# A two-layer attention and FFN kernel: residual kept token-major, layernorm transposed by DMA, heads spread over the partitions, attention weights spread by selector matmuls

## The chip, the cores and the metric

The kernel runs on one core of one Trainium2 chip. The metric is the time of one execution on the device, in microseconds (us). "Median" is the median over the runs of one kernel. "Span" is the time from the first to the last instruction in the one profiled execution, which is some 1 to 2 us shorter than the time of that run.

Engines in the profile: PE is TensorE's matmuls, PEld its weight loads (they overlap PE), DVE is VectorE, ACT is ScalarE, POOL is GpSimd, SP is SyncE, which here only starts DMAs.

## The reference

Two layers. Each is a sliding-window attention block followed by an FFN, each with a layernorm in front and a residual around it. There are 2048 tokens, width 1024, 32 heads of 32, a window of 8 keys at distances 0, 2, ..., 14, and an FFN width of 3584. Everything is bf16.

```python
def _A_ref(x, wqkv, wo):                       # B=1, S=2048, D=1024, H=32, Dh=32
    qkv = (x @ wqkv).reshape(B, S, 3, H, Dh).transpose(2, 0, 3, 1, 4)
    q, k, v = qkv[0], qkv[1], qkv[2]
    idx = pos[:, None] - (jnp.arange(8) * 2)[None, :]
    # kg, vg: rows idx of k and v; idx < 0 is masked
    logits = einsum("bhsd,bhswd->bhsw", q, kg) * Dh ** -0.5
    o = einsum("bhsw,bhswd->bhsd", softmax(logits), vg)
    return o.transpose(0, 2, 1, 3).reshape(B, S, D) @ wo

def _B_ref(x, w1, b1, w2, b2):                 # F=3584
    return gelu(x @ w1 + b1) @ w2 + b2

for layer in range(2):                         # written out twice in the reference
    x = x + _A_ref(layernorm(x), A_wqkv, A_wo)
    x = x + _B_ref(layernorm(x), ...)
```

## The kernel before

Tokens go through in groups of 512. There are four groups and two layers, so eight steps `n`. The program is a software pipeline: the attention of step `n` is spread as "sides" between the FFN matmuls of step `n-1`.

The residual `xg` is feature-major: features lie on the partitions and tokens along the free axis. Three things follow. The input must be transposed by TensorE. The output must be transposed back. And the mean and the variance of a token are sums over partitions, which the kernel makes with matmuls against a tile of ones:

```python
def load_x_tile(g, tl):                        # input: 8 identity transposes on TensorE
    ...
    for c in range(KD):
        m = tr(pst[:, c, :], xin[:, c * P:(c + 1) * P], ident[:])
    nc.scalar.copy(xg[g][:, :, tl * P:(tl + 1) * P], pst[:])
# store_x_tile does the same on the way out

class LN:
    def s1a(self):                             # the mean
        if self.presum: ...                    # 8 planes added on VectorE first, then one matmul
        else:
            for c in range(KD):
                m = mm(self.tot[...], lhsT=ones_bf[:], rhs=x[:, c, ...], start=(c == 0), stop=(c == KD - 1))
    # s1b subtracts the mean; s2a squares on ScalarE and sums again with ones_bf; s3 multiplies by rstd
```

The columns of Q, K and V come in the order of the weights, so a 128-row chunk `c` holds four whole heads. The product of the attention weights with V therefore needs, for each chunk, a tile in which the weights of each of its four heads stand on 32 partitions. The kernel writes the weights to DRAM and reads them back by broadcast DMAs, 1 MB for each chunk, issued from GpSimd and tied to TensorE's progress:

```python
def av_a(n, c):
    ...
    for hi in range(HPC):                      # 4 DMAs of 256 KB for each chunk
        src = a_d[HPC * c + hi:HPC * c + hi + 1, :, :].rearrange("o w t -> o (w t)").to_broadcast([DH, W * T])
        d = ABC_Q.dma_start(abc[hi * DH:(hi + 1) * DH, :, :].rearrange("p w t -> p (w t)"), src)
        if mark[0] is not None:
            dep_sync(d, mark[0], "pace abc broadcast with PE progress")
    nc.vector.tensor_tensor(out=abc[:], in0=abc[:], in1=win(vT[:, c, :]), op=ALU.mult)
# av_b_dve then adds the 8 window positions in three halving steps into oT[:, c, :]
```

One AV chunk is placed every five chunks of FFN1 (in the last of the eight steps, every three):

```python
u_list = [1 + 5 * c for c in range(NCH)]
# ... sides of gen_ffn1(n - 1); the last two chunks go into gen_ffn2(n - 1)
```

Of the kernel before, what the change touches and what calls it, by code (L numbers as in the profile page):

```python
# [8 lines left out]
ACT = mybir.ActivationFunctionType  # L9
# [5 lines left out]
DRAM = bass.MemoryType.DRAM  # L15
# [3 lines left out]
def kernel(  # L19
# [11 lines left out]
):  # L31
    nc = tc.nc
# [12 lines left out]
    NQ = 4  # L45
    TB = T // NQ
    NTT = T // P
    assert DH == 32 and P // DH == 4 and H * NQ == P
    assert S % T == 0 and D % (4 * P) == 0 and F % (4 * P) == 0
# [3 lines left out]
    KH = KF // 2  # L53
    HPC = P // DH
    NCH = D // P
    NSTEP = NLAYER * NG
    LN_SET = "natural_log_exp_and_others"
    N_FFN1 = KF
    N_FFN2 = (KD // 2) * 4
    N_QKV = 3 * NCH  # L60
# [4 lines left out]
    wo_v = A_wo.rearrange("(k p) f -> p k f", p=P)  # L65
# [5 lines left out]
    wpool = ctx.enter_context(tc.tile_pool(name="wpool", bufs=4))  # L71
    lnp = ctx.enter_context(tc.tile_pool(name="lnp", bufs=1))
    xnp = ctx.enter_context(tc.tile_pool(name="xnp", bufs=2))
    attp = ctx.enter_context(tc.tile_pool(name="attp", bufs=1))
    qp = ctx.enter_context(tc.tile_pool(name="qp", bufs=2))
    prodp = ctx.enter_context(tc.tile_pool(name="prodp", bufs=3))
    smp = ctx.enter_context(tc.tile_pool(name="smp", bufs=1))
    abcp = ctx.enter_context(tc.tile_pool(name="abcp", bufs=3))
    iop = ctx.enter_context(tc.tile_pool(name="iop", bufs=2))
    psum = ctx.enter_context(tc.tile_pool(name="psum", bufs=1, space=PSUM))  # L80
    dram = ctx.enter_context(tc.tile_pool(name="dram", bufs=2, space=DRAM))
    pools = {"hpool": None, "abcx": None, "abcx_cm": None}

    def acc_tile():
        return psum.tile([P, T], F32, name="acc", bufs=4)

    def aux_f32():
        return psum.tile([P, T], F32, name="aux", bufs=2)

    def aux_tr():  # L90
        return psum.tile([P, KD, P], BF16, name="aux", bufs=2)

    def dep_sync(dependent, dependency, why):
        tc.add_manual_dep(dependent.ins, dependency.ins.name,
                          mybir.DependencyInfo(mybir.DependencyClass.Sync, mybir.DependencyReason.SCHED_ONLY), reason=why)
# [5 lines left out]
    last_pe = [None]  # L101
    mark = [None]

    ABC_Q = nc.gpsimd

    PIN_MODE = 0
    VFIRST = False
    PE_AV = False
    ONE_AHEAD = True
    RED_BATCH = 2  # L110
    PRESUM = True
    PRESUM_B = False
    DMA_XPOSE = False
    OT_BUFS = 1 if ONE_AHEAD else 2
    LN_TILED = False
    last_seg = [None]

    def pe_chain(inst, seg):
        if last_pe[0] is not None:
            if PIN_MODE == 1 or (PIN_MODE == 2 and seg != last_seg[0]):  # L120
                dep_order(inst, last_pe[0], "PE program order")
        last_pe[0] = inst
        last_seg[0] = seg
        return inst

    def _seg(out_ap):
        return (out_ap.tensor.name, out_ap.offset)

    def mm(out_ap, *args, **kwargs):
        return pe_chain(nc.tensor.matmul(out_ap, *args, **kwargs), _seg(out_ap))  # L130

    def tr(out_ap, *args, **kwargs):
        return pe_chain(nc.tensor.transpose(out_ap, *args, **kwargs), out_ap.tensor.name)  # L133

    xg = [xpool.tile([P, KD, T], BF16, name=f"xg{g}") for g in range(NG)]
    def load_x(g):
        d = nc.sync.dma_start_transpose(xg[g][:], x_in[g * T:(g + 1) * T, :].rearrange("s (k p) -> s k p", p=P))
        if mark[0] is not None:
            dep_sync(d, mark[0], "keep the x load at its program position")

    def load_x_tile(g, tl):
        xin = iop.tile([P, D], BF16, name="xio")
        d = nc.sync.dma_start(xin[:], x_in[g * T + tl * P:g * T + (tl + 1) * P, :])
        if mark[0] is not None:
            dep_sync(d, mark[0], "keep the x load at its program position")
        pst = aux_tr()
        for c in range(KD):
            m = tr(pst[:, c, :], xin[:, c * P:(c + 1) * P], ident[:])
            if c == 0 and mark[0] is not None:
                dep_order(m, mark[0], "keep the input transposes at their program position")  # L150
        nc.scalar.copy(xg[g][:, :, tl * P:(tl + 1) * P], pst[:])

    if DMA_XPOSE:
        load_x(0)

    ident = const.tile([P, P], BF16, name="ident")
    make_identity(nc, ident[:])
    ones_bf = const.tile([P, P], BF16, name="ones_bf")
    nc.vector.memset(ones_bf[:], 1.0)
    eps_t = const.tile([P, 1], F32, name="eps_t")  # L160
    nc.vector.memset(eps_t[:], EPS)
    q32 = const.tile([P, P], BF16, name="q32")
    nc.vector.memset(q32[:], 1.0 / 32.0)
    smat = const.tile([P, NCH, H], BF16, name="smat")
    nc.gpsimd.memset(smat[:], 0.0)
    for c in range(NCH):
        for hi in range(HPC):
            m = HPC * c + hi
            nc.gpsimd.memset(smat[hi * DH:(hi + 1) * DH, c, m:m + 1], 1.0)
    maskrow = const.tile([1, W, 16], BF16, name="maskrow")  # L170
    nc.gpsimd.memset(maskrow[:], 0.0)
    for wp_ in range(W):
        nmask = HALO - DIL * wp_
        if nmask > 0:
            nc.gpsimd.memset(maskrow[0:1, wp_, 0:nmask], -1e9)
    onesrow = const.tile([1, H], BF16, name="onesrow")
    nc.gpsimd.memset(onesrow[:], 1.0)
    b1_bf = const.tile([P, KF], BF16, name="b1_bf")
    b2_bf = const.tile([P, KD], BF16, name="b2_bf")
    b1T = const.tile([P, KF], F32, name="b1T")  # L180
    b2T = const.tile([P, KD], F32, name="b2T")

    def load_bias():
        with nc.allow_non_contiguous_dma(reason="tiny bias loads"):
            d1 = nc.gpsimd.dma_start(b1_bf[:], B_b1.rearrange("(j p) -> p j", p=P))
            d2 = nc.gpsimd.dma_start(b2_bf[:], B_b2.rearrange("(j p) -> p j", p=P))
        if mark[0] is not None:
            dep_sync(d1, mark[0], "keep the bias load at its program position")
            dep_sync(d2, mark[0], "keep the bias load at its program position")
        nc.vector.tensor_copy(b1T[:], b1_bf[:])  # L190
        nc.vector.tensor_copy(b2T[:], b2_bf[:])
# [3 lines left out]
    nc.gpsimd.memset(zhalo[:], 0.0)  # L195

    def store_x_tile(g, tl):
        pst = aux_tr()
        for c in range(KD):
            tr(pst[:, c, :], xg[g][:, c, tl * P:(tl + 1) * P], ident[:])  # L200
        xo = iop.tile([P, D], BF16, name="xio")
        nc.scalar.copy(xo[:], pst[:].rearrange("p c t -> p (c t)"))  # L202
        nc.sync.dma_start(out_v[g * T + tl * P:g * T + (tl + 1) * P, :], xo[:])

    def rstd_from(src, prev, preload, c0=0, c1=T):
        rstd = lnp.tile([P, T], F32, name="rstd", bufs=2)
        if preload:
            pl = nc.scalar.preload_act_table_set(LN_SET)
            dep_order(pl, prev, "table preload after squares")
            prev = pl  # L210
        ln_i = nc.scalar.activation(rstd[:, c0:c1], src, ACT.Ln, bias=eps_t[:], scale=1.0 / D)
        dep_order(ln_i, prev, "ln after squares/preload")
        nc.scalar.activation(rstd[:, c0:c1], rstd[:, c0:c1], ACT.Exp, scale=-0.5)  # L213
        return rstd

    class LN:
        def __init__(self, g, preload=False, cols=None, xn=None, presum=False):
            self.g = g
            self.xn = xn
            self.preload = preload  # L220
            self.presum = presum
            self.c0, self.c1 = cols if cols is not None else (0, T)

        def _pin(self, m):
            if mark[0] is not None:
                dep_order(m, mark[0], "keep LN matmuls at their program position")

        def _partial(self, rhs_of):
            c0, c1 = self.c0, self.c1
            pq = aux_f32()  # L230
            for c in range(KD):
                j = c % 4
                m = mm(pq[j * 32:(j + 1) * 32, c0:c1], lhsT=ones_bf[:, 0:32], rhs=rhs_of(c),
                       start=(c < 4), stop=(c >= KD - 4), tile_position=(0, j * 32))
                if c == 0:
                    self._pin(m)
            hi = lnp.tile([P, T], BF16, name="hi", bufs=1)
            nc.scalar.copy(hi[:, c0:c1], pq[:, c0:c1])
            lo = lnp.tile([P, T], BF16, name="lo", bufs=1)
            nc.vector.tensor_tensor(out=lo[:, c0:c1], in0=pq[:, c0:c1], in1=hi[:, c0:c1], op=ALU.subtract)  # L240
            return hi, lo

        def _combine(self, hi, lo):
            c0, c1 = self.c0, self.c1
            tot = aux_f32()
            m = mm(tot[:, c0:c1], lhsT=q32[:], rhs=hi[:, c0:c1], start=True, stop=False)
            self._pin(m)
            mm(tot[:, c0:c1], lhsT=q32[:], rhs=lo[:, c0:c1], start=False, stop=True)
            return tot
# [609 lines left out]
```

## Time and profile before

| | before |
|---|---|
| median, 3 runs | 1432.17 us (1431.49 to 1435.05) |
| span of the profiled run | 1427.0 us |
| PE busy | 1327.6 us (93%) |
| first GELU of FFN1, group 0 | 217.9 us after the start |
| from there to the end | 1209.1 us |

These are lines of the page of the kernel before. First comes the span, then busy time by engine. The two digit rows give busy tenths in 40 slices of the span. Then come two DMA queues with packets, MB and their share of the 16 DMA engines' time, and one kind of DMA with its size and its median time to landing.

```profile
span 1427.0 us, 15506 instructions
...
PE 1327.6 (93%) x6473; PEld 595.5 (42%) x6602; DVE 743.1 (52%) x604; ACT 426.1 (30%) x670; POOL 149.5 (10%) x339
...
PE   4978279999999999999999999999999999799998
...
DMA  4366728973799449983699638993599738964551
...
q1 hardware_dynamic: 245120, 192.95, 48.0%
q0 software_dynamic: 13424, 69.23, 22.1%
...
abc<-a_d POOLq DMA_DIRECT2D x256, 256.0 KB, 8.4
```

TensorE is full (a 9 in nearly every slice) except in the first six slices, some 214 us, where the digits are 4, 9, 7, 8, 2, 7. The queue of the broadcasts, q0, takes 22.1% of all DMA time.

The next line is a stretch of 25 us in a steady FFN1. Its columns are length, busy time and count of PE, PEld, DVE, ACT and POOL, granted clock, DMA share, GB/s.

```profile
250.00:275.00 25.00, 24.84 (x115) 11.37 (x116) 6.07 (x7) 6.18 (x9) 5.79 (x12) 1.00 1.10 238
```

115 matmuls of 512 columns in 24.84 us are 0.216 us each. The program has 5632 such projection and FFN matmuls, so some 1217 us are fixed. The DMA share adds up packet times over 16 engines, so it can pass 1; 1.10 reads as all 16 engines taken while the broadcasts ran.

The waits of TensorE, longest in total first (total us, number of times, longest):

```profile
PE acc L130 <- ACT vT L412: 27.3, 1, 27.3
PE aux L133 <- DMA xio<-in_A_x_dram: 24.2, 6, 9.8
PE acc L130 <- DMA wt<-in_B_w_dram: 11.2, 2, 8.1
PE aux L130 <- ACT sq L295: 9.3, 12, 5.2
```

The timeline of TensorE before its first FFN1 matmul (start, length, what, how often, and in brackets the idle time just before and what ended it):

```profile
143.74 4.93 PE L130 MATMUL acc<-xn,wt 128*128 128x512 bf16 x18 [0.22 <-issue]
176.00 8.63 PE L130 MATMUL acc<-xn,wt 128*128 128x512 bf16 x31 [27.33 <-ACT vT L412]
```

The hole from 149 to 176 us is a wait for a V copy on ScalarE. That copy writes the one `vT` buffer, which the AV chunks of the group before still read. A wait costs more than its length: the 31 matmuls after the hole took 8.63 us, where 31 times 0.216 are 6.7 us, and the granted clock from 176 to 184 us was 0.77.

### The profile page before, as it was taken

The page shows a single profiled execution, that of the slowest core. Times are in us where ns is not written, and L with a number is a line of the kernel's source. Part 1 is how long each engine was busy: PE and PEld are TensorE (multiplying, and loading weights), DVE is VectorE, ACT ScalarE, POOL GpSimd, SP SyncE. Part 2 cuts the span into 40 slices and gives each one's busy share as a digit, 9 for nine tenths or more (in the row PEclk, how much of TensorE's full clock was granted, in tenths as well). Part 3 has the DMA queues.
Part 4 walks back from the last instruction along what each step waited for, and adds up shares of the span by engine and source line. Part 5 has one row for each costly group of instructions (what it writes and reads, how often), then busy time and mean ns, then how long its engine had stood idle before and what let it go on. Part 6 is the DMA issues. An engine that isn't in the chain of part 4 may idle for free.

```text
span 1427.0 us, 15506 instructions
## 1 busy us (share of the span) xinstructions
PE 1327.6 (93%) x6473; PEld 595.5 (42%) x6602; DVE 743.1 (52%) x604; ACT 426.1 (30%) x670; POOL 149.5 (10%) x339
## 2 busy tenths in 40 slices
PE   4978279999999999999999999999999999799998
PEld 2433124444444444444444444444444444344443
DVE  2556834386436773386444774286644773742001
ACT  3433123123432044123431144223431234202411
POOL 1020302100121002100121002200121002200000
PEclk8998589999999999999999999999999999999999
DMA  4366728973799449983699638993599738964551
GB/s 154 101 190 194 172 89 212 244 194 118 203 243 240 148 134 246 227 226 118 189 226 222 193 111 224 239 234 135 162 252 238 210 104 222 255 176 150 173 152 59
DMA packets 258613, 263.17 MB, mean 184 GB/s; under 512 B 8176, under 2 KB 245744, under 8 KB 250352
## 3 DMA queue, kind: packets, MB, share of 16 engines
q1 hardware_dynamic: 245120, 192.95, 48.0%
q0 software_dynamic: 13424, 69.23, 22.1%
q8 instruction: 51, 0.84, 0.3%
q14 instruction: 18, 0.15, 0.0%
HBM read 255.86 MB, written 6.29 MB: 184 GB/s over the span
## 4 chain that ended last, share of the span: by engine, by line
PE 86%; DMA 7%; DVE 4%; issue 1%; ACT 1%; another core or an unknown queue 0%; POOL 0%; SPq 0%; DVEq 0%; POOLq 0%; ACTq 0%
PE acc L130 79%; DMA wt<-in_B_w_dram 4%; DMA xio<-in_A_x_dram 3%; PE aux L130 3%; PE L L130 2%; DVE abc L476 1%; PE aux L133 1%; DVE xn L283 1%; ACT sq L295 0%; DVE abc L483 0%; ACT xio L202 0%; DVE abc L484 0%; DVE xn L330 0%; DMA abc<-a_d 0%; DVE prod L444 0%
## 5 line engine op out<-in xcount | busy, mean ns | idle before, releaser
L130 PEld LDWEIGHTS <-wt 128*128 128x128 bf16 x5632 | 549.1, 98 | 727.6 <-issue 76.4
L130 PE MATMUL acc<-xn,wt 128*128 128x512 bf16 x3247 | 742.5, 383 | 46.6 <-ACT vT L412 27.3
L130 PE MATMUL acc<-hT,wt 128*128 128x512 bf16 x1756 | 390.3, 380 | 4.8 <-DMA wt<-in_B_w_dram 3.1
L476 DVE TENSOR_TENSOR abc<-abc,vT 128x4096 bf16<-128x4096 bf16 x64 | 146.4, 2288 | 204.1 <-DMA abc<-a_d 192.1
L524 ACT ACTIVATE hT<-acc,b1T 128x512 bf16<-128x512 f32 x224 | 153.9, 687 | 264.4 <-PE acc L130 256.5
L444 DVE TENSOR_TENSOR prod<-qT,kT 128x4096 bf16<-128x4096 bf16 x64 | 145.9, 2289 | 100.9 <-ACT kT L440 100.9
L473 POOL DMA_DIRECT2D abc<-a_d x256 | 124.0, 493 | 518.6 <-PE acc L130 289.2
L295 ACT ACTIVATE sq<-xn 128x512 bf16<-128x512 bf16 (+1 forms) x136 | 75.4, 598 | 227.6 <-DVE xn L283 188.8
L130 PE MATMUL acc<-oT,wt 128*128 128x512 bf16 x502 | 113.1, 379 | 1.5
L330 DVE TENSOR_TENSOR xn<-xn,rstd 128x2048 bf16<-128x2048 bf16 (+1 forms) x34 | 73.2, 2161 | 27.4 <-ACT rstd L213 27.4
L437 ACT CAST qT<-acc 128x512 bf16<-128x512 f32 x64 | 37.4, 584 | 144.4 <-PE acc L130 144.3
L483 DVE TENSOR_TENSOR abc<-abc 128x2048 bf16<-128x2048 bf16 x64 | 78.3, 1223 | 1.7
L400 POOL DMA_DIRECT2D a_d<-a x32 | 18.5, 611 | 575.1 <-DVE a L397 575.1
L545 DVE SCALAR_TENSOR_TENSOR xg_96<-acc,b2T,xg_96 128x512 bf16<-128x512 f32 x16 | 12.0, 749 | 113.0 <-PE acc L130 110.7
L440 ACT CAST kT<-acc 128x512 bf16<-128x512 f32 x64 | 37.2, 581 | 66.7 <-PE acc L130 63.3
L412 ACT CAST vT<-acc 128x512 bf16<-128x512 f32 x64 | 37.0, 584 | 59.5 <-PE acc L130 58.4
L484 DVE TENSOR_TENSOR abc<-abc 128x1024 bf16<-128x1024 bf16 x64 | 44.1, 690 | 1.8
L202 ACT COPY xio<-aux 128x1024 bf16<-128x1024 bf16 x16 | 16.0, 1010 | 90.3 <-PE aux L133 85.2
L130 PE MATMUL aux<-sq,ones_bf 128*128 128x512 bf16 (+1 forms) x88 | 32.5, 392 | 9.3 <-ACT sq L295 9.3
L133 PE MATMUL aux<-ident,xio 128*128 128x128 bf16 x128 | 12.0, 254 | 27.9 <-DMA xio<-in_A_x_dram 24.2
L130 PE MATMUL L<-prod,smat 128*32 128x512 bf16 x512 | 37.5, 383 | 0.4
L130 PEld LDWEIGHTS <-ones_bf 128*128 128x128 bf16 x188 | 19.0, 101 | 34.3 <-issue 16.0
(89 smaller groups left out, 405.1 us busy)
## 6 DMA issues: line engine op xcount, KB each, us to landing
abc<-a_d POOLq DMA_DIRECT2D x256, 256.0 KB, 8.4
wt<-in_B_w_dram SPq DMA_DIRECT2D x56, 1024.0 KB, 5.7
wt<-in_B_w_dram SPq DMA_DIRECT2D x64, 896.0 KB, 11.2
wt<-in_A_wqkv_dram SPq DMA_DIRECT2D x48, 1024.0 KB, 5.0
wt<-in_A_wo_dram SPq DMA_DIRECT2D x16, 1024.0 KB, 8.0
xio<-in_A_x_dram SPq DMA_DIRECT2D x16, 256.0 KB, 3.0
out_dram<-xio SPq DMA_DIRECT2D x16, 256.0 KB, 2.0
a_d<-a POOLq DMA_DIRECT2D x32, 64.0 KB, 2.2
```

The costliest lines, as they stand in the source:

```text
L130: return pe_chain(nc.tensor.matmul(out_ap, *args, **kwargs), _seg(out_ap))
L295: self.last_sq = nc.scalar.activation(sq[:, c0:c1], xn[:, c, c0:c1], ACT.Square)
L330: nc.vector.tensor_tensor(out=xn[:, hh * KH2:(hh + 1) * KH2, c0:c1], in0=xn[:, hh * KH2:(hh + 1) * KH2, c0:c1], in1=rstd[:, c0:c1].unsquee ...
L412: nc.scalar.copy(vT[:, c, HALO:], psv[:])
L437: nc.scalar.copy(qT[:], psq[:])
L440: nc.scalar.copy(kT[:, c, HALO:], psk[:])
L444: nc.vector.tensor_tensor(out=prod[:], in0=qT[:].unsqueeze(1).to_broadcast([P, W, T]), in1=win(kT[:, c, :]), op=ALU.mult)
L473: d = ABC_Q.dma_start(abc[hi * DH:(hi + 1) * DH, :, :].rearrange("p w t -> p (w t)"), src)
L476: nc.vector.tensor_tensor(out=abc[:], in0=abc[:], in1=win(vT[:, c, :]), op=ALU.mult)
L483: nc.vector.tensor_tensor(out=pv[:, 0:4, :], in0=pv[:, 0:4, :], in1=pv[:, 4:8, :], op=ALU.add)
L484: nc.vector.tensor_tensor(out=pv[:, 0:2, :], in0=pv[:, 0:2, :], in1=pv[:, 2:4, :], op=ALU.add)
L524: nc.scalar.activation(hT[:, j, :], ps[:], ACT.Gelu_apprx_tanh, bias=b1T[:, j:j + 1])
```

## The change

The intent is to take everything off TensorE that is no projection, and the broadcast off the DMA engines.

- The residual is token-major. Loads and stores need no transpose. Mean and variance of a token lie along the free axis (`bn_stats` on VectorE). The normalised tile goes through one DMA transpose.
- The columns of Q, K and V are taken with a step of 8 (`c::NCH`), so that every 128-row chunk holds 4 rows of each of the 32 heads. The tile of attention weights is then the same for all eight chunks of a group.
- That one tile is made on chip: eight matmuls against a 0/1 selector and eight ScalarE copies for each group of tokens, in place of 8 MB of broadcasts.
- The weight pool goes from 4 to 6 buffers, and TensorE's accumulators in PSUM from 4 to 6. Group 0 gets its own `vT` buffer. The AV chunks stand three FFN1 chunks apart, not five. FFN2 and the output projection swap operands, so that their results come out token-major.

```diff
-    wpool = ctx.enter_context(tc.tile_pool(name="wpool", bufs=4))
+    wpool = ctx.enter_context(tc.tile_pool(name="wpool", bufs=6))
...
-    wo_v = A_wo.rearrange("(k p) f -> p k f", p=P)
+    wo_v = A_wo.rearrange("(p c) f -> p c f", c=NCH)
...
+    def ln_tile(t, tt, xnT):
+        stats = lnp.tile([P, 2, 6], F32, name="stats")
+        for h in range(2):
+            nc.vector.bn_stats(stats[:, h, :], x[t][:, h * HALF:(h + 1) * HALF])
+        ...                                    # bn_aggr; rstd with two small POOL operations
+        nc.vector.tensor_scalar(out=xn[:], in0=x[t][:], scalar1=mv[:, 0:1], scalar2=rstd[:], op0=ALU.subtract, op1=ALU.mult)
+        nc.sync.dma_start_transpose(xnT[:, tt, :, :], xn[:].rearrange("s (k p) -> s k p", p=P))
...
+    def qkv_chunk(wts, c, xnT):
+        ps = acc_tile()
+        for k in range(KD):
+            mm(ps[:], lhsT=wts[k // (KD // 2)][:, k % (KD // 2), c::NCH], rhs=xnT[:, :, k, :], start=(k == 0), stop=(k == KD - 1))
...
+    def spread(n):
+        ...
+        for wh in range(2):
+            for tb in range(NTT):
+                ps = acc_tile()                # six accumulators in all
+                mm(ps[:], lhsT=selbc[tb * H:(tb + 1) * H, :], rhs=a[tb * H:(tb + 1) * H, wh * 4:(wh + 1) * 4, :],
+                   start=True, stop=True, tile_position=(tb * H, 0))
+                nc.scalar.copy(abc[:, wh * 4:(wh + 1) * 4, tb * P:(tb + 1) * P], ps[:].rearrange("p (w t) -> p w t", w=4))
...                                            # av(n, c): product with the one abc, then the same halving adds
+    mk_ln_a(0)                                 # the start
+    add(sides, 0, lambda: load_x(1))
+    add(sides, 4, lambda: mk_ln_a(1))
+    run(gen_qkv(0), sides)
+    add(sides, 1, lambda: spread(0))
+        add(sides, 2 + c, lambda c=c: av(0, c))
+    add(sides, 12, lambda: mk_ln_a(2))
+    run(gen_qkv(1), sides)
+    run(gen_wo(0))
...                                            # then, for each later group:
+        add(sides, 1, lambda: spread(n))
+            add(sides, 2 + 3 * c, lambda c=c: av(n, c))
+        run(gen_ffn1(n - 1), sides)
```

## The prediction

> **What bounds the kernel now.** TensorE. The page shows PE busy 1327.6 of 1427.0 us. The groups list 5632 weight loads for the projection and FFN matmuls (128x512). The stretches table has 115-116 of them per 24.9 us when steady, 0.216 us each; the Trainium skill, "TensorE: Matmul & The Clock Gate", Back-to-back issue gap, gives 512/2.4 + 2.5 = 216 ns, and the trace agrees. So 5632 x 0.216 = 1215 us is a floor that the change keeps. The rest, about 212 us, is mainly the start: FFN1 begins at 214 us (timeline), though only 448 matmuls (97 us) and two score reductions (9 us) must precede it; PE's waits show 24 us for x loads and one of 27 us at 149-176 us for the attention weights' broadcast. Then 35 us of layernorm ones-matmuls, 9 us of output transposes, 11 us of weight-DMA waits, a 10 us tail, 24 us of score reductions.
>
> **What the change removes.** Ones-matmuls and identity transposes on PE; the squares on ACT (75 us, hidden); the 69 MB broadcast (22% of DMA time; 8.4 us to landing); the 4.4 us VectorE subtractions. w2 rows become 1 KB instead of 512 B; the weight pool goes from 4 to 6.
>
> **What it adds.** 64 selector matmuls, four in one array pass: about 4 us on PE; 64 ACT copies of about 0.58 us (hidden, but six accumulators for eight spreads stall PE about 1 us per group). 64 crossbar transposes of 256 KB: the skill, "DMA: Bandwidth & Descriptors", Latency and other measured facts, has 261 GB/s, so an estimated 1 us of transfer, perhaps 3-4 us to landing. No trace here shows one yet. bn_stats, an estimated 0.7 us each, from a 512-column VectorE operation. A second FFN2 add. Q/K weights are read with a step of 8 columns; I expect no slowdown, since a load (98 ns) hides behind a 216 ns matmul twice over.
>
> **Critical path.** Steady groups stay PE-bound: in the K stage a product costs 2.29 us on VectorE against 1.73 + 0.5 us on PE, lag two; the eight AV chunks need 37 us inside FFN1's 48 us. Layernorm and transposes have a whole stage of slack. The start stays slow: layernorm plus transposes behind weight loads put the first projection at about 25 us (31 before); VectorE's order puts layernorm of group 2 ahead of the first products (about 8 us stall); in the second QKV six AV chunks stand before the first product, so that stage takes about 75 us instead of 48 (25 us stall); then about 8 us of exposed layernorm before FFN1. FFN1 begins near 180 us instead of 214. From there 5184 x 0.216 + 24 + 12 + tail 5 + stray stalls 20 = 1180 us instead of 1213.
>
> **Predicted:** 1360 us, 8-in-10 range 1332 to 1402. Faster by over 2%: 0.87; within 2%: 0.08; slower by over 2%: 0.05.
>
> **What would show it.** PE about 95% busy; projection matmuls still 0.216 us apart in every stage, Q and K included; no abc DMA; FFN1 of group 0 beginning at 165-195 us; the largest single PE wait before then, on a product; waits after 200 us under 30 us in all; tail under 6 us.
>
> **What would make it wrong.** Strided weight loads slower than 216 ns; transposes taking 10 us or more or holding the SyncE queue so that weights come late; VectorE order delaying products in every group, not only in the second.

## More of the kernel before

The GELU writes the tile `hT`. Its tile view (count, shortest/median/longest ns, first and last start) gives a clean mark between the start and the rest:

```profile
L524 ACT ACTIVATE hT<-acc,b1T x224: 687/687/688, 217.9 to 1369.5; 128x512 bf16<-128x512 f32 x112
```

In all, the view of TensorE's waits lists 71.4 us before the first GELU. The chain that ended last shows what this window was made of. First it hangs on input loads (`xio`), then on AV products (`abc`) one after another, 4.65 us apart:

```profile
98.28 12.23 DMA xio<-in_A_x_dram
...
149.63 2.30 DVE abc L476
...
154.28 2.29 DVE abc L476
```

## The result, and the profile after

A ratio below is the mean time of one kernel's runs over that of the other's of the same rounds, with its 95% interval. It is therefore not quite the ratio of the medians.

| | before | after |
|---|---|---|
| median, 4 runs each | 1431.83 us | 1352.10 us |
| ratio | 1 | 0.9437 (0.9397 to 0.9476) |
| span | 1427.0 us | 1350.7 us |
| first GELU of FFN1 | 217.9 us | 178.7 us |
| from there to the end | 1209.1 us | 1172.0 us |

The changed kernel is 5.6% faster and correct. Of 76.3 us of span, 39.2 us came before the first GELU and 37.1 us after it.

The page after, the same lines as before, with the DMA transposes in place of the broadcasts:

```profile
span 1350.7 us, 14693 instructions
...
PE 1285.6 (95%) x6222; PEld 628.1 (46%) x6222; DVE 722.0 (53%) x809; ACT 329.3 (24%) x530; POOL 56.0 (4%) x158
...
PE   2893979999999999999999999999999999999998
...
DMA  9740554554645544555645545456464654466440
...
q1 hardware_dynamic: 218752, 209.74, 51.3%
q0 software_dynamic: 160, 0.27, 0.2%
...
xnT<-xn SPq DMA_TRANSPOSE x64, 4.2
```

The queue of the broadcasts is nearly empty (0.2%, the bias loads). The DMA row never shows more than a 6 after the first slices, where it used to show 8 and 9. The same stretch of steady FFN1 now reads

```profile
190.00:215.00 25.00, 25.00 (x117) 11.30 (x116) 25.00 (x24) 9.36 (x14) 0.00 (x0) 1.00 0.39 122
```

The spacing of the matmuls is unchanged, the DMA share fell from 1.10 to 0.39, and VectorE is now the busy one in this stretch (25.00 of 25.00 us, and 34.3 of the 45.1 us from 182.6 to 227.7), where the AV chunks stand closer. The waits of TensorE, all of them:

```profile
PE acc L87 <- DMA xnT<-xn: 31.8, 2, 24.8
PE L L87 <- DVE big L220: 24.6, 4, 14.7
PE acc L87 <- ACT hT L308: 1.7, 7, 0.2
```

That is all the view lists. No wait for weights is left, and all but the last line lie before FFN1. The timeline shows where:

```profile
24.78 20.77 PE L87 MATMUL acc<-xnT,wt 128*128 128x512 bf16 x88 [24.78 <-DMA xnT<-xn]
49.52 1.04 PE L87 MATMUL L<-big,smat 128*32 128x512 bf16 x8 [3.97 <-DVE big L220]
...
86.13 15.70 PE L87 MATMUL acc<-xnT,wt 128*128 128x512 bf16 x72
116.56 1.04 PE L87 MATMUL L<-big,smat 128*32 128x512 bf16 x8 [14.72 <-DVE big L220]
...
175.41 5.00 PE L87 MATMUL acc<-xnT,wt 128*128 128x512 bf16 x16 [7.00 <-DMA xnT<-xn]
180.35 0.60 PE L87 MATMUL acc<-a,selbc 32*128 32x512 bf16 x5
181.19 1.33 PE L87 MATMUL acc<-a,selbc 32*128 32x512 bf16 x3 [0.24 <-ACT hT L308]
182.64 45.05 PE L87 MATMUL acc<-xnT,wt 128*128 128x512 bf16 x208
```

In order: 24.8 us until the first transposed tile is there; 4.0 us for the first score product of group 0; 14.7 us for one of group 1, which stands on VectorE behind AV chunks of group 0; 7.0 us of layernorm and transpose before FFN1. The 27 us hole of before is gone. The second `vT` buffer is not the reason: the last AV chunk of group 0 ended at 129.5 us, before the first V copy of group 1 at 141.2 us.

The start as a whole is not simply rid of waits. The view lists 56.4 us of them before the first GELU, where it was 71.4 us: 15.0 us fewer. The other 24 of the 39.2 us are, by subtraction, what TensorE no longer does there (64 ones-matmuls, half of them of 256 columns, and 128 input transposes) and the slower passes after waits; no run separates these. The GELU's tile view:

```profile
L308 ACT ACTIVATE hT<-acc,b1T x224: 678/687/782, 178.7 to 1298.3; 128x512 bf16<-128x512 f32 x112
```

**A ledger of the 37 us after the first GELU.** From the kernel before it removes 124 ones-matmuls of 512 columns, at 0.216 us 26.8 us. It removes 96 of the 128 output transposes (the other 32 lie in the tail), at the 73 ns that 9.4 us busy over 128 give, 7.0 us. It removes 11.2 us of waits for weights. The tail after the last FFN2 matmul goes from 9.4 us (1417.6 to 1427.0) to 4.1 us (1346.6 to 1350.7), another 5.3 us. It adds selectors: seven groups of 2.3 us (the timeline above, 180.35 to 182.64), 16 us. That makes 26.8 + 7.0 + 11.2 + 5.3 - 16 = 34 us of the 37 us. Some 3 us stay unplaced.

### The profile page after: what moved, and what is told of

Its sections match the earlier page's. It is cut to its first block, busy times and chain, and to the rows that moved or that the text cites. A ratio compares the mean times of both kernels' runs of the same rounds, so it can differ in the third digit from the quotient of the medians.

```text
span 1350.7 us, 14693 instructions
## 1 busy us (share of the span) xinstructions
PE 1285.6 (95%) x6222; PEld 628.1 (46%) x6222; DVE 722.0 (53%) x809; ACT 329.3 (24%) x530; POOL 56.0 (4%) x158
## 3 DMA queue, kind: packets, MB, share of 16 engines
q1 hardware_dynamic: 218752, 209.74, 51.3%
## 4 chain that ended last, share of the span: by engine, by line
PE 90%; DVE 4%; ACT 2%; DMA 1%; issue 0%; POOL 0%; SPq 0%; DVEq 0%; ACTq 0%
PE acc L87 87%; PE L L87 3%; DVE big L268 1%; ACT abc L261 1%; DVE big L269 1%; DVE big L220 0%; DVE stats L143 0%; DMA xnT<-xn 0%; ACT hT L308 0%; DVE big L270 0%; DMA x_93<-in_A_x_dram 0%; DVE xn L150 0%; SPq L151 0%; POOL rstd L148 0%; DVE oT L271 0%
## 5 line engine op out<-in xcount | busy, mean ns | idle before, releaser
L87 PE MATMUL acc<-xnT,wt 128*128 128x512 bf16 x3328 | 743.0, 383 | 32.7 <-DMA xnT<-xn 31.8
L87 PEld LDWEIGHTS <-wt 128*128 128x128 bf16 x3328 | 391.5, 120 | 383.4 <-issue 67.0
L87 PE MATMUL acc<-wt,hT 128*128 128x512 bf16 x1792 | 388.1, 379 | 0.0
L87 PEld LDWEIGHTS <-hT 128*128 128x128 bf16 x1792 | 175.3, 98 | 211.4
L327 DVE TENSOR_TENSOR tmp<-acc,b2bc 128x512 f32<-128x512 f32 x64 | 44.3, 692 | 393.9 <-PE acc L87 389.5
L220 DVE TENSOR_TENSOR big<-qT,kT 128x4096 bf16<-128x4096 bf16 x64 | 143.0, 2286 | 44.6 <-ACT kT L218 43.7
L268 DVE TENSOR_TENSOR big<-abc,vT 128x4096 bf16<-128x4096 bf16 x64 | 143.7, 2285 | 28.9 <-ACT abc L261 28.9
L87 PE MATMUL acc<-wt,oT 128*128 128x512 bf16 x512 | 111.8, 379 | 0.0
L87 PEld LDWEIGHTS <-oT 128*128 128x128 bf16 x512 | 50.1, 98 | 60.3
L269 DVE TENSOR_TENSOR big<-big 128x2048 bf16<-128x2048 bf16 x64 | 75.4, 1218 | 0.0
```

The costliest lines, as they stand in the source:

```text
L87: inst = nc.tensor.matmul(*args, **kwargs)
L220: nc.vector.tensor_tensor(out=prod[:], in0=qT[:, c, :].unsqueeze(1).to_broadcast([P, W, T]), in1=win(kT[:, c, :]), op=ALU.mult)
L268: nc.vector.tensor_tensor(out=pv[:], in0=s["abc"][:], in1=win(s["vT"][:, c, :]), op=ALU.mult)
L269: nc.vector.tensor_tensor(out=pv[:, 0:4, :], in0=pv[:, 0:4, :], in1=pv[:, 4:8, :], op=ALU.add)
L327: nc.vector.tensor_tensor(out=tmp[:], in0=pss[tt][:], in1=b2bc[:, dh * HALF:(dh + 1) * HALF], op=ALU.add)
```

## The experiments

The theory, T: after the start, TensorE's stream of instructions sets the time, and each 512-column pass costs 0.216 us whatever its operands are. The gain there is the passes taken out, less the selectors. At the start, T expects the gain from the end of the waits. The rivals:

- R1: the gain is DMA relief. The removed 69 MB of broadcasts (or the deeper weight pool) let the weights come in time.
- R2: the gain is relief of VectorE and ScalarE.
- Against the change itself: the strided weight loads, or the DMA transposes, cost time that hides a larger gain.

Twelve kernels ran, in four calls, each on one chip with runs of the kernel before beside it (its medians there: 1429.51, 1428.91, 1433.47 and 1429.04 us). All were correct except two.

| run | median us | ratio to before (95%) | span | first GELU | rest |
|---|---|---|---|---|---|
| before | 1431.83 | 1 | 1427.0 | 217.9 | 1209.1 |
| after | 1352.10 | 0.9437 (0.9397 to 0.9476) | 1350.7 | 178.7 | 1172.0 |
| e1 ones-matmuls out of before | 1410.75 | 0.9874 (0.9850 to 0.9899) | 1412.0 | 218.3 | 1193.7 |
| e2 contiguous columns | 1351.67 | 0.9453 (0.9426 to 0.9479) | 1345.8 | 174.5 | 1171.3 |
| e3 weight pool of 4 | 1346.35 | 0.9423 (0.9397 to 0.9449) | 1344.2 | 172.2 | 1172.0 |
| e4 broadcast back, packed | 1460.17 | 1.0230 (1.0173 to 1.0288) | 1472.1 | 180.2 | 1291.9 |
| e5 broadcast back, old pace | 1399.28 | 0.9798 (0.9749 to 0.9847) | 1392.6 | 208.1 | 1184.5 |
| e6 transposes on TensorE | 1376.90 | 0.9636 (0.9597 to 0.9674) | 1374.7 | 172.1 | 1202.6 |
| e7 spread by DMA | 1353.69 | 0.9471 (0.9438 to 0.9503) | 1350.1 | 194.0 | 1156.1 |
| e8 spread in halves | 1344.73 | 0.9410 (0.9378 to 0.9442) | 1343.1 | 178.7 | 1164.4 |
| e9 start reordered | 1342.86 | 0.9357 (0.9313 to 0.9401) | 1341.7 | 169.2 | 1172.5 |
| e10 start, AV order, hybrid | 1320.51 | 0.9208 (0.9176 to 0.9239) | 1319.4 | 164.3 | 1155.1 |
| e11 before without broadcast | 1376.31 | 0.9626 (0.9602 to 0.9651) | 1373.2 | 179.9 | 1193.3 |
| e12 best | 1317.52 | 0.9216 (0.9192 to 0.9239) | 1315.5 | 157.5 | 1158.0 |

### e1: take most ones-matmuls out of the kernel before

The kernel before can add the eight planes on VectorE first and leave one matmul of eight. It does so for the layernorm in front of attention. This run does it for the one in front of the FFN, in six steps, 14 passes each.

```diff
-    PRESUM_B = False
+    PRESUM_B = True
```

> The kernel before with one flag turned: in six of the eight second layernorms the 16 ones-matmuls become 2, and VectorE does the sums instead (about 5 us more VectorE work per group). Theory T (TensorE's instruction stream sets the time after the start; every 512-column pass taken off it is worth 0.216 us): 84 passes fewer, 18 us, so 1414 us or a ratio near 0.987. Rival R2 (the gain of the change came from relieving VectorE and ScalarE): no change or a slowdown, ratio 1.00 or more.

84 passes at 0.216 us are 18.1 us. The median fell by 18.8 us, the part after the first GELU by 15.4 us, and the start did not move (217.9 to 218.3). The additions went to VectorE, which got busier by the page (771.7 us, 743.1 before), so R2 fails for this term. The price of a pass is confirmed within these two figures: TensorE's stream sets the time there.

### e2: contiguous columns for Q, K and V (a wrong result)

```diff
-  lhsT=wts[k // (KD // 2)][:, k % (KD // 2), c::NCH]
+  lhsT=wts[k // (KD // 2)][:, k % (KD // 2), c * P:(c + 1) * P]
```

> The changed kernel with Q, K and V columns taken as contiguous blocks of 128 instead of every eighth column; the result is wrong on purpose, the work is the same. T: the weight loads of those stages fall from about 0.14 us to about 0.10 us each, but they hide behind 0.216 us matmuls, so 1352 us within 4 us. Rival (the strided loads cost TensorE time): at least 10 us faster.

The group of weight loads (busy us and mean ns of one; idle time and what ended it) in the changed kernel, and then in e2:

```profile
L87 PEld LDWEIGHTS <-wt 128*128 128x128 bf16 x3328 | 391.5, 120 | 383.4 <-issue 67.0 <-DMA xnT<-xn 7.5
```

```profile
L87 PEld LDWEIGHTS <-wt 128*128 128x128 bf16 x3328 | 322.3, 98 | 447.4 <-issue 68.8 <-DMA xnT<-xn 7.4
```

Of the 3328 loads 1536 are strided, so 69.2 us over 1536 are 45 ns more for each: 143 ns against 98 ns. The median did not move (1351.67 against 1352.10 us), nor did the part after the first GELU (1171.3 against 1172.0 us). The profiled run began FFN1 4 us earlier, which the medians do not repeat: so much can one profile's start differ without an edit to it. A load of 143 ns still hides behind a matmul of 216 ns. Only where eight K matmuls follow a score reduction do they take 1.88 us, against 1.83 us in e2; 48 such places make some 2 us by estimate, too little for the medians to show. The Trainium skill, "TensorE: Matmul & The Clock Gate", section "Weight-path perf modes - Fast Weight Load (FWL) and DoubleRow", allows that mode a column step up to 1,024 elements and reads its chunks "packed or strided". No run here shows whether these loads use the mode. That loads with a step of 8 give right results the changed kernel shows, and the trace adds that the step costs 45 ns.

### e3: the weight pool back to four buffers

```diff
-    wpool = ctx.enter_context(tc.tile_pool(name="wpool", bufs=6))
+    wpool = ctx.enter_context(tc.tile_pool(name="wpool", bufs=4))
```

> The changed kernel with 4 weight buffers as before instead of 6. T: with DMA engines about half busy the weights still come in time: 1352 us within 5 us, PE waits on weights under 5 us. Rival R1 (part of the gain came from the deeper pool): at least 10 us slower, with waits of PE on the weight tile.

After the first GELU there is no difference at all (1172.0 us in both), and TensorE waits for no weights. The deeper pool is therefore no part of the gain. The start is 6.5 us shorter (172.2 against 178.7), in part because the first score reduction no longer waits 3.97 us for a product:

```profile
45.62 0.62 PE L87 MATMUL L<-big,smat 128*32 128x512 bf16 x8 [0.53 <-POOL rstd L147]
```

The first matmul came 1.2 us earlier too (23.6 us). That fewer weight loads then stand ahead of the x loads is my inference, which no run takes apart. Some 4 us of start can differ between profiles (e2), but here the medians differ by 5.75 us as well, and the times of the two kernels do not overlap.

### e4: the broadcast put back, at the changed kernel's AV cadence

The changed kernel with the old traffic beside it: 1 MB of broadcasts for each AV chunk, into a tile that nothing reads, paced like the old ones. It has four weight buffers (e3 has shown that those cost nothing after the start).

```diff
+        dump = dumpp.tile([P, W, T], BF16, name="dump")
+        rows = B_w2.rearrange("(r f) d -> r (f d)", f=4)
+        for hi in range(4):
+            d = nc.gpsimd.dma_start(dump[hi * DH:(hi + 1) * DH, :, :].rearrange("p w t -> p (w t)"),
+                                    rows[4 * c + hi:4 * c + hi + 1, :].to_broadcast([DH, W * T]))
+            dep_sync(d, last_pe[0], "pace the extra broadcast with PE progress")
```

> The changed kernel with 4 weight buffers, plus the DMA traffic that the change took out: 256 broadcasts of 256 KB, paced by TensorE, into a buffer that nobody reads. T: the DMA share returns to 70 to 80 percent, and the cost is at most what the kernel before shows as waits on weights, 0 to 12 us. Rival R1 (the gain came from relieving the DMA engines): 30 us or more of the 80 come back, as PE waits on weight tiles.

The time rose by some 114 us, above the kernel before. The start hardly moved (180.2), but 119.9 us were lost after it (the profiled run was the slowest of four, 13.7 us above the median). T expected next to nothing and missed. TensorE's longest wait is

```profile
PE acc L92 <- DMA wt<-in_B_w_dram: 80.4, 21, 7.5
```

The AV chunks of the changed kernel stand three FFN1 chunks apart, so 1 MB of broadcast is wanted every 5.2 us (three chunks of eight passes) while the FFN wants 1 MB of weights every 6.9 us. The kernel before asks for the broadcast every 8.6 us, except in its last group. So this run tests the old bytes at a pace that the old kernel has for one group of eight. There the old kernel pays as well: its broadcasts are issued 5.2 us apart (1197.0, 1202.2, 1207.4 us), and at 1237.4 us comes its longest wait for weights, 8.1 of its 11.2 us. Both show that with the broadcast the tight AV cadence makes weights late. But e4 doesn't price the broadcast in the kernel before.

### e5: the broadcast put back at the old pace

As e4, but with the broadcasts issued one per five FFN1 chunks, as in the kernel before:

```diff
+        add(sides, 2 * c, lambda c=c: bcast(c))            # second QKV
+            if c < 6:
+                add(sides, 1 + 5 * c, lambda c=c: bcast(c))  # FFN1; chunks 6 and 7 in FFN2 at 1 and 4
```

> As the run with the broadcasts put back (4 weight buffers, 256 unread broadcasts of 256 KB), but one 1 MB set per five FFN1 chunks (8.6 us), the pace of the kernel before, instead of one per three (5.2 us). T: the 110 us of the first version came from packing the traffic too densely beside the weight loads; at the old pace the waits on weights are 0 to 20 us, as the 11 us of the kernel before, so 1346 to 1366 us against 1346 for 4 buffers alone. Rival R1 (the removed traffic was a large part of the gain at its own pace too): 30 us or more slower than that.

Against e3, the same kernel without the traffic, the start grew by 35.9 us (172.2 to 208.1) and the rest by 12.5 us (1172.0 to 1184.5). The waits show it:

```profile
PE acc L92 <- DMA xnT<-xn: 38.0, 2, 24.1
...
PE acc L92 <- DMA wt<-in_A_wo_dram: 19.4, 2, 17.1
PE acc L92 <- DMA wt<-in_B_w_dram: 8.9, 5, 2.7
```

T had allowed 0 to 20 us and missed, for it had counted only the steady waits for weights and left out the start, where x tiles, Q/K/V weights and broadcasts meet. R1, which I had counted as a rival, is a large part of the truth.

### e6: the transposes done by TensorE, not by DMA

```diff
-        nc.sync.dma_start_transpose(xnT[:, tt, :, :], xn[:].rearrange("s (k p) -> s k p", p=P))
+        tq.append((tick[0], (xn, tt, xnT)))     # taken up three chunks later by:
+    def tr_tile(xn, tt, xnT):
+        pst = psum.tile([P, KD, P], BF16, name="acc", bufs=6)
+        for k in range(KD):
+            inst = nc.tensor.transpose(pst[:, k, :], xn[:, k * P:(k + 1) * P], ident[:])
+            ...                                 # tied into PE's order like every matmul
+        nc.scalar.copy(xnT[:, tt, :, :], pst[:])
```

The weight pool has 5 buffers here and the `xn` pool 5.

> The changed kernel with the 64 DMA transposes replaced by 8 identity matmuls each into an accumulator bank and one ScalarE copy, issued three chunks later so that TensorE need not wait for the layernorm; 5 weight buffers to make room. T: 64 times 0.46 us (what 8 identity transposes take in the stream of the kernel before) is 30 us more TensorE stream, a few us less at the start where transposes queued behind weights: 1370 to 1385 us. Rival (the DMA transposes cost as much themselves): 1352 us or less.

```profile
PE acc L110 <- ACT xnT L114: 4.8, 10, 0.7
...
15.40 13.97 PE L88 MATMUL acc<-xnT,wt 128*128 128x512 bf16 x64 [1.30 <-ACT xnT L114]
```

Of the 512 transposes of 128x128, 384 lie after the first GELU, and the part after it grew by 30.6 us. 4.8 us of that are waits for ScalarE's copies between them, by the view of TensorE's waits. The other 25.8 us are 67 ns a transpose. The DMA transposes thus earn some 30 us there. The first projection, however, came at 15.4 us and not at 24.8 us, and the first GELU 6.6 us earlier. That is not the price of the DMA transposes alone, since this run also has five `xn` buffers and five weight buffers: e9 keeps the DMA transposes, has four of each and holds the bias loads back, and its first projection comes at 17.5 us; e3, with four weight buffers only, has the same first GELU (172.2 against 172.1 us). That leaves some 2 us at the first projection for the way over the DMA engines, by a comparison of kernels that differ in more than this.

### e7: the attention weights spread by DMA, not by selectors

The head-spread layout would also let a DMA make the one tile: four DMAs to DRAM, then four of 256 KB back, per group, 1 MB in place of 8 MB.

```diff
-                mm(ps[:], lhsT=selbc[...], rhs=a[...], ...)
-                nc.scalar.copy(abc[...], ps[:]...)
+        for j in range(HP):
+            nc.gpsimd.dma_start(abc[j::HP, :, :], a[:])     # a is now a tile in DRAM
```

> The changed kernel with the selector matmuls undone: the softmax weights go to DRAM and come back as four loads of 256 KB per group, each row to every fourth partition. The head-spread column order stays, so one 1 MB broadcast serves all eight chunks instead of 8 MB as before. T: TensorE's stream loses about 2.2 us in each of 8 groups, of which 7 are where TensorE never waits: 14 to 18 us faster, near 1336 us. Rival (the selector matmul is what hides the latency): AV late, waits of TensorE on oT, 1352 us or more.

After the first GELU 15.9 us are gone, 2.27 us for each of seven groups: that is what the selectors cost. At the start, however, the way over DRAM takes longer. The AV chunks of group 0 begin at 97.7 us instead of 88.6, and the score products of group 1, which stand behind them on VectorE, make TensorE wait longer:

```profile
PE acc L89 <- DMA xnT<-xn: 38.2, 2, 24.6
PE L L89 <- DVE big L222: 36.3, 3, 27.2
```

The start grew by 15.3 us and the net is nothing (1353.69 against 1352.10 us).

### e8: the selectors in two halves

```diff
-        add(sides, 1, lambda: spread(n))
+        add(sides, 1, lambda: spread(n, (0,)))
+        add(sides, 2, lambda: spread(n, (1,)))
```

> The changed kernel with each group's eight selector matmuls cut into two fours, one FFN1 chunk apart. T: eight spreads on six accumulator banks hold TensorE for 2.2 us of which about 1.1 us is array time in two passes with their drain; halves leave ScalarE time to empty the banks, so 1.0 us per group comes back: 6 to 9 us faster, near 1344 us, and the wait on the accumulators (idle before the second part of the selectors) is gone. Rival: the 2.2 us are the selectors' own array time, no gain.

Four selectors now take four of the six accumulators, and a chunk of FFN1 lies between the two halves. The timeline of the fourth group's FFN1 in e8:

```profile
498.85 0.40 PE L87 MATMUL acc<-a,selbc 32*128 32x512 bf16 x4
499.18 1.90 PE L87 MATMUL acc<-xnT,wt 128*128 128x512 bf16 x8
501.01 0.51 PE L87 MATMUL acc<-a,selbc 32*128 32x512 bf16 x4
```

A half now takes 0.4 to 0.5 us (four matmuls in hardly more than the 0.38 us of one), where eight in one go took 2.3 us with an accumulator wait inside (the timeline after the change, above: five, a gap, then three stretched over 1.33 us). The part after the first GELU fell by 7.6 us, the start did not move. So about half of the selectors' price was a queue for accumulators, not matmul time.

### e9: the start reordered

```diff
-    wpool ... bufs=6        # also: xn pool 2 -> 4
+    wpool ... bufs=4
+        dep_sync(d, last_pe[0], "keep the bias loads at their program position")
-    add(sides, 12, lambda: mk_ln_a(2))
```

> The changed kernel with four edits that touch only the start: the bias loads held back to late in the first QKV stage, four xn buffers instead of two (so that a layernorm tile need not wait for the transposes before it), four weight buffers, and the third group's layernorm left to the FFN2 stage. T (what is left of the start is VectorE order and queueing, about 45 us of waits): the first projection at about 18 us instead of 24.8, no 4 us wait on the first product, the first GELU at about 165 us instead of 178.7, the part after it unchanged at 1172 us: 1338 us. Rival (the start is bound by DMA bytes): first GELU within 4 us of 172, as with 4 buffers alone.

```profile
PE acc L91 <- DMA xnT<-xn: 27.0, 2, 17.5
```

The four buffers are meant to keep a group's four transposes from waiting for one another's. The first matmul came at 17.5 us (24.8 before) and the first product wait is gone; which of the four edits did it, the run can't say (e3 had ended that product wait with the smaller weight pool alone). But the first GELU came only at 169.2 us, with the median at 1342.86 us where I had expected about 165 and 1338: the wait for layernorm before FFN1 grew from 7.0 to 9.5 us, and the 14.7 us product wait is untouched. By the mark set beforehand, "within 4 us of 172", this is the rival's result, not T's. Yet the first projection did come 6 us earlier than in e3, and 2.5 us of that were lost again in the longer wait for layernorm, so that the start is bound by DMA bytes is not shown either.

### e10: also the AV order, and the DMA spread where it is hidden

```diff
-        add(sides, 2 + c, lambda c=c: av(0, c))
+        add(sides, (2, 3, 11, 12, 13, 14, 15, 16)[c], lambda c=c: av(0, c))
+        for j in range(HP if n > 0 else 0):     # DMA spread, as in e7, for all groups but the first
+            nc.gpsimd.dma_start(abc[j::HP, :, :], a[:])
```

> On top of the reordered start: in the second QKV stage the products come before most of the AV chunks on VectorE, and the groups after the first spread their weights by DMA, while the first, where TensorE waits for it, keeps the selector matmuls. T: the part after the first GELU falls to about 1156 us as in the run with all spreads by DMA, and the first GELU comes at about 157 us: 1315 us, a ratio near 0.92. Rival: the two do not add, because late DMA spreads meet the weight loads: 1325 us or more.

Six of the eight AV chunks of group 0 now stand behind the first score products of group 1. The wait of 14.7 us is gone (products: 11.5 us in three waits, the longest 5.7 us), and so are the selectors of the later groups: 1155.1 us after the first GELU, the shortest of all. The first GELU, however, came at 164.3 us and not at the expected 157, and the median is 1320.51 us, between T's 1315 and the rival's 1325: 16.2 us of wait for the layernorm's transposes before FFN1 had appeared, where it was 9.5 us in e9. In that stretch VectorE's softmax, the third group's statistics and GpSimd's DMA issues stand between the small operations of the layernorm. That they cause it is read from the order of the trace.

### e11: the kernel before without its broadcast (a wrong result)

The direct test of R1: nothing else of the change, only the broadcast taken out. The AV product reads a constant tile (to make room for it, the pool of AV tiles goes from 3 to 2 buffers). One product of group 0 then runs before the group's softmax is done (82.5 against 89.0 us); the other seven still stand behind it in VectorE's order.

```diff
-        for hi in range(HPC):
-            ...
-            d = ABC_Q.dma_start(abc[hi * DH:(hi + 1) * DH, :, :].rearrange("p w t -> p (w t)"), src)
-        nc.vector.tensor_tensor(out=abc[:], in0=abc[:], in1=win(vT[:, c, :]), op=ALU.mult)
+        nc.vector.tensor_tensor(out=abc[:], in0=cst[:], in1=win(vT[:, c, :]), op=ALU.mult)
```

> The kernel before with its 256 broadcasts taken out and a constant in place of the attention weights; the result is wrong on purpose. It shows what the broadcast (traffic and wait together) costs where it stood. T: at the start the 27 us wait goes and the first GELU comes at 180 to 190 us instead of 217.9, since the waits for x and the layernorm sums remain; after it, the 11 us of waits on weights go, 1209 becomes 1196 to 1200 us: 1380 to 1390 us in all, half of the 80 us. Rival R1 (the broadcast is nearly the whole gain): 1360 us or less.

```profile
L521 ACT ACTIVATE hT<-acc,b1T x224: 680/687/689, 179.9 to 1315.7; 128x512 bf16<-128x512 f32 x112
```

The first GELU came at 179.9 us (217.9 before), and the rest took 1193.3 us (1209.1 before): this one removal gives 38.0 + 15.8 = 53.8 us, where the whole change gives 76.3 us. The V-copy wait of 27.3 us is 1.3 us here, and the waits for x loads fell from 24.2 to 11.0 us. The median, 1376.31 us, lies between T's 1380 to 1390 and R1's 1360 or less: T's share for the broadcast was somewhat too small, and R1 in its strong form, nearly the whole gain, fails. This agrees with e5, which put the traffic back from the other side and lost 35.9 and 12.5 us. The removal here also ends the wait for the DRAM round trip of the weights, so what e11 takes away is the broadcast as a whole, its landing time and its traffic together. Before the first GELU the view lists 36.4 us of waits in e11, 71.4 us in the kernel before and 56.4 us in the changed one: of the start's relief the changed kernel gives 20 us back, as its own waits for the first transposes and for products.

### e12: the version that beats both

e10, with selectors also for group 1 (so that the DMA issues leave the start), and with the statistics of the third group's layernorm held back to their place in the program.

```diff
+        for j in range(HP if n > 1 else 0):
+            nc.gpsimd.dma_start(abc[j::HP, :, :], a[:])
+        for wh in range(2 if n <= 1 else 0):
...
+            b = nc.vector.bn_stats(stats[:, h, :], x[t][:, h * HALF:(h + 1) * HALF])
+            if hold:
+                dep_sync(b, last_pe[0], "keep this layernorm at its program position")
```

> As the run with products first and DMA spreads, with two repairs of what that run showed before the first FFN1 (a 16.2 us wait on the transposes): the third group's layernorm is held back on VectorE by a wait on TensorE's progress, and the second group also keeps the selector spread, so that its loads do not stand between the layernorm's small operations on GpSimd. T: that wait falls to 8 to 10 us, the selectors cost 2.2 us: first GELU near 157 us instead of 164.3, 1157 us after it: 1314 us. Rival: the wait is the VectorE softmax and stays, 1320 us or more.

```profile
PE acc L93 <- DMA xnT<-xn: 25.6, 2, 16.9
PE L L93 <- DVE big L230: 11.1, 3, 5.7
```

1317.52 us, correct: 7.8% under the kernel before and 2.6% under the changed one by the medians. The first GELU came at 157.5 us (157 expected), the rest took 1158.0 us (1157 expected). The wait before FFN1 is 8.8 us where e10 had 16.2, which supports the reading of e10, though two repairs went in at once and their shares stay open. e10 and e12 ran in different calls, and their ratios (0.9208 and 0.9216) don't separate them: e12 starts FFN1 earlier and pays one more group of selectors.

## Why the prediction was right, and where its steps were not

The time was 1352.1 us where 1360 was predicted, and the direction and the range held. Half of the miss lies before FFN1 (180 said, 175.4 us measured), half after it (1180 said, 1175.3 us). The sums came nearer than their terms, and that is in part luck: at the start the named terms were 9.6 us too large together and the sum only 4.6, and after it stalls set too high made up for selectors set too low. By point:

- **TensorE bounds, and 0.216 us a pass is kept in every stage.** Right but for the K stage, where eight passes between two score reductions take 1.88 us, not 1.73 (timeline below), and for the first passes after a wait. In the second Q stage the 72 matmuls with strided loads run at (15.70 - 0.38) / 71 = 0.216 us, taking 0.38 us as the length of one. The Trainium skill, "TensorE: Matmul & The Clock Gate", section "Back-to-back issue gap", gives 216 ns by the formula that the prediction cites, and this trace agrees. PE is 95% busy, as said.
- **Ones-matmuls and transposes off TensorE are worth their passes.** Right for the ones-matmuls: e1 measured 15.4 to 18.8 us for 84 passes worth 18.1 us. The transposes of the kernel before were not taken out alone; e6 prices others, at 67 ns each.
- **Strided loads cost nothing.** Right about the time (e2). "About 98 ns" for a load was wrong: 143 ns.
- **DMA transposes: 3 to 4 us to landing.** 4.2 us median. After the start TensorE never waits for them by the view of its waits, and e6 is no faster without them.
- **The start: FFN1 near 180 us, between 165 and 195.** 175.4 us. Its terms, predicted and measured: first projection 25 and 24.8 us; first-product stall 8 and 4.0 us; stall in the second QKV 25 and 14.7 + 0.2 + 5.7 = 20.6 us; exposed layernorm 8 and 7.0 us. The sizes of the two product stalls were over-estimated. And the first one went away in e3, where only the weight pool is smaller, so VectorE's order, which the prediction names, can't be its whole cause (e2 shortens it too, to 1.6 us, without an edit to the start).
- **"The largest single PE wait before then, on a product."** Wrong. The largest is the very first, 24.8 us for the transposes. The product wait of 14.7 us comes second. The prediction had those 25 us in its own sum and forgot them when it named the sign to look for.
- **Selectors "about 4 us on PE" and a stall of "about 1 us per group", 12 us in all.** Mis-sized. e7 measured 2.27 us a group, 15.9 us for seven groups. e8 showed that 7.6 us of that go when the eight are split, so the stall part was about right (8 us) and the matmul part too small.
- **"Stray stalls 20" from FFN1 on.** There were 1.4 us of traced waits after 200 us. The whole stretch took 1175.3 us where 1180 was said. With 5184 passes at 0.216 us (1119.7), six groups of score reductions at eight times 0.55 us (26.4), selectors 15.9, and the tail 4.1, about 9 us remain. The timeline of a K stage places most of them:

```profile
57.57 1.95 PE L87 MATMUL acc<-xnT,wt 128*128 128x512 bf16 x8
59.45 0.62 PE L87 MATMUL L<-big,smat 128*32 128x512 bf16 x8
```

  Eight projection passes take 1.88 us from their start to the start of the score reduction, where 8 x 0.216 are 1.73 us; in the fourth group it is the same (469.25 to 471.13 us). Eight such places in each of six groups make some 7 us, as an estimate. The 16 matmuls at 175.4 us, the first after a wait, took 4.9 us to the next start, some 1.5 us more than 16 x 0.216. The prediction priced each pass alone and had no term for going from one kind to the other and back.
- **The tail under 5 us, waits under 30 us after 200 us, no broadcast DMA.** Right: 4.1 us, 1.4 us, none.

What the prediction did not say is how much of all this hung on the broadcast. It lists the 27 us wait and the 11 us of weight waits, but treats the ones-matmuls and the new layout as equals of it. e11 shows that taking out the broadcast alone gives 53.8 us, where the whole change gives 76.3. The remaining 22.5 us are, by subtraction, the net of fewer passes and a shorter tail, less the selectors and the start's new waits. That split depends on the order in which parts are removed: e4 shows how strongly the cadence of the AV chunks and the traffic act on each other.

The rivals, then: R1 holds for the larger part, as relief at the start above all (38.0 of 53.8 us), but not as a deeper pool (e3). T holds for the steady stream (e1, e6, e7, e8). R2 is not supported: VectorE's work hardly fell (743.1 to 722.0 us), and e1 adds to it and gains. ScalarE's fell more (426.1 to 329.3 us); no run tests that alone, but after the first GELU TensorE waited for ScalarE only 2.7 us in all in the kernel before, by the view of its waits, all of it at the output copies. The worry about strided loads fell with e2, the worry about transposes with e6; in the first 25 us they cost some 2 us by the unclean comparison of e6 and e9.

## What to carry to other kernels

When one engine is full in the steady part, look at the start apart from it: here half of the gain, and more than half of what e12 still won (21 of 35 us), lay before the first FFN matmul, much of it in waits that a share over the whole span does not show. Price a removed matmul by the spacing of the stream, and a removed DMA by what it collides with, and test the second by removing it alone, for putting it back at another pace tests something else. A batch that wants more accumulators than there are stalled the full engine here (eight for six, 7.6 us over seven groups); splitting it helped.

## What the Trainium skill lacked or had wrong

- "TensorE: Matmul & The Clock Gate", section "Back-to-back issue gap": it calls N/2.4 + 2.5 an isolated gap that over-counts in a stream, and gives some 131 ns per 512-column matmul for a sustained one. Here the sustained spacing is 0.216 us wherever no score reduction stands between, with a weight load for each matmul (117 in 25.0 us in a steady stretch). The formula fits the stream; 131 ns was never seen.
- The same page, section "Weight-path perf modes - Fast Weight Load (FWL) and DoubleRow": it doesn't say that a column step of 8 makes the load longer, 143 ns against 98 ns (e2), which hides behind a 512-column matmul.
- The same page, "Part 4: PE-mode transpose": it gives some 390 ns alone and some 275 ns in a kernel. These are durations of one, and the kernel before shows 254 ns on average for its own. What the page lacks is the cost in a full stream: 384 of them took 25.8 us, 67 ns each, or 80 ns with the waits for the copies (e6).
- "DMA: Bandwidth & Descriptors", section "Latency and other measured facts": it has 261 GB/s for DMA transposes. Here a 256 KB transpose from SBUF to SBUF landed 4.2 us after issue. As an estimate from the page lines, the hardware queue's share was 51.3% of 1350.7 us with the 64 transposes and 43.3% of 1374.7 us without (e6), a difference of 98 us of all 16 engines, so 1.5 us each or some 171 GB/s, while weight loads ran beside them. The page's figure is for "non-contiguous mid-dim"; it has no time from issue to landing of a transpose.
- No page that I found tells what a broadcast stream and a weight stream do to one another: 1 MB of broadcasts every 5.2 us beside 1 MB of weights every 6.9 us gave 80.4 us of waits for weights (e4), while at the pace of one per five chunks it was 8.9 us for the same weights (e5). As an estimate, a 1 MB broadcast takes 4.9 us of all 16 engines (22.1% of 1427.0 us over 64). So e4 asks for 0.95 of the engines beside the weights' 0.39 (the stretch after the change), more than there is, and the old pace for 0.57 beside 0.39.
